# AM, KB and GL on VectorE alone, the first weights' words loaded at the start, and a reordered set-up in a planned recurrence-plus-FFN kernel

## The chip, the cores and the metric

The kernel runs on one core of a Trainium2 chip. The metric is device time in microseconds; several executions are timed and the median is given. One further execution was profiled, and every row below comes from it.

## The reference, cut to what matters

A recurrence over 768 steps for 4 x 8 independent heads with a 40 x 40 state, and two feed-forward layers over its 3072 output rows:

```python
for t in range(S):                       # S = 768, D = 40, B = 4, H = 8
    y[:, :, t] = einsum('bhd,bhde->bhe', r_t, state)
    Sa = einsum('bhde,bhe->bhd', state, a_t)
    state = state * w_t[:, :, None, :] - outer(Sa, b_t) + outer(v_t, k_t)
x = y.transpose(0, 2, 1, 3).reshape(3072, 320)
h = x @ w_in;  g = h * tanh(softplus(h)); x = g @ w_out      # 320 -> 2048 -> 320
h = x @ w_in2; g = h * cos(h);            out = g @ w_out2   # 320 -> 2048 -> 320
```

The weights arrive as 64-bit numbers, and are converted on the chip from their two 32-bit words.

## The kernel before, in words

The recurrence is cut into chunks of 32 steps. There are 48 chunks (`TOT`), numbered g: two halves of 16 heads, 24 chunks each. For each chunk there are four pieces of work.

- `pre(g)`: load `IN` (two DMAs), scan the decays on VectorE into `PE` (L662), take the reciprocal and scan back into `RP` (L667, L668), form `AM` (two products, L676) and `KB` (two products, L682), zero the other halves of `AM` on GpSimd (L689), multiply `AM` by `KB` on TensorE (L698), mask the result back into `AM` on VectorE (L708), and store the strictly triangular systems to DRAM (`l_d`, L721). `IN` has two buffers, `RP` and `KB` one.
- `inverse_two`: the systems of one to three chunks are read back with heads on partitions, and solved by 14 dependent pairs of VectorE instructions (L779 multiplies into `XT`, L777 adds into `XM`; both inputs of each lie in SBUF). The result goes to DRAM (`t_d`) and comes back as `TT`; `halves` joins the 16 x 16 blocks with `lowd` and `lowm`, two constants made in set-up. The first chunk alone uses `TMP` in place of `XM`.
- `chain(g)`: the serial part: small matmuls, evictions by ScalarE and VectorE (L708, L951, L978, L986), the state for the next chunk, and the output `Y`. Every fourth chunk stores a block of 256 rows to `x_d`.
- `prep` (first layer's weights): 17 loads of 512 KB of raw words into the five buffers `RW` (slices of `TMP`), two ScalarE instructions and four VectorE instructions of 128 x 512 each (L460 to L476), then a split into a high and a low part (`wih` and `wil`, L381 and L506); 5 further loads follow when `TMP` is given up.

`layer1(blk)` needs the output of chunk 4 blk + 3: it splits `XR` into `XH` (ScalarE, L1123) and `XL` (VectorE, L1125), runs the first product (L1068), the activation twice into `H` and `GH` (L1140, L1142), their difference `GL` (L1145), and the second product (L1049). There are 64 + 32 `GL` instructions. `layer2` does the same with another activation (its `GL` is L1231, on GpSimd). Its first two blocks have 256 rows, the others 512.

The order of the instructions of each engine is not written by hand. `Plan.run` is a list scheduler in Python: each piece is a `Task` with an engine or a choice of engines, an assumed duration, predecessors, buffers (`ring`) that it takes and frees, and a priority (`prio`, smaller goes first). The scheduler simulates the engines, and emits the instructions in the order in which it started the tasks. On the chip each engine then runs its list in that order, and waits by semaphores. `port=True` on a task says that VectorE and GpSimd tasks so marked are not planned at the same time. The planner has no bandwidth for DMA: it assumes a load to be there 2.6 to 4.1 us after its issue. Chains have the first priority (-10000 + 10 g), set-up apart; then inverses and `pre` (-5000 + 10 g); then the weights (-4921); then the layers (0 and up). All DMAs are issued by SP in one list.

What the change touches: `AMKB` and `GLE` are `("POOL", "DVE")`, so that the planner chooses GpSimd or VectorE for each; `B_G` biases that choice for GL; `W1_AFTER` makes all weight loads wait for the store of chunk 1's systems (`ldma[1]`); the list at L1263 hands out the five `RW` buffers, three of them after inverses of the first batches have been stored. In set-up, GpSimd does `setup_g` (constants, identity, masks), `setup_x` (zeroes `XM`) and `setup_tf` (`lowd`, and `lowm` as 16 additions one after the other) ahead of all other GpSimd work.

Of the kernel before, what the change touches and what calls it, by code (L numbers as in the profile page):

```python
# [14 lines left out]
ALU = mybir.AluOpType  # L15
# [31 lines left out]
       ("POOL", "POOL"): 0.1, ("POOL", "DVE"): 0.08, ("POOL", "PE"): 0.1, ("POOL", "ACT"): 0.1}  # L47
SLACK = {"PE": 0.02, "DVE": 0.02, "ACT": 0.02, "POOL": 0.2, "SP": 0.02}

EARLY = (20.0, 0.3)  # L50


class Task:
    __slots__ = ("eng", "dur", "fn", "preds", "acq", "rel", "aset", "lat", "prio", "end", "n_wait", "succ", "ready", "cols", "engs", "takes", "name", "durs", "bias", "ffn", "port", "mode", "soft")

    def __init__(self, eng, dur, fn, preds=(), acq=(), rel=(), aset=None, lat=None, prio=0.0, cols=0.0, bias=BIAS, port=False):
        self.bias = bias
        self.ffn = cols > 0 and prio >= 0
        self.cols = cols
        self.engs = (eng,) if isinstance(eng, str) else eng  # L60
        self.takes = fn.__code__.co_varnames[:1] == ("eng",)
        self.name = fn.__qualname__.replace("body.<locals>.", "").replace("<locals>.", "")
        self.durs = dict(zip(self.engs, dur if isinstance(dur, tuple) else (dur,) * len(self.engs)))
        dur = self.durs[self.engs[0]]
        self.eng, self.dur, self.fn, self.preds = self.engs[0], dur, fn, [p for p in preds if p is not None]
        self.acq, self.rel, self.aset, self.lat, self.prio = list(acq), list(rel), aset, lat, prio
        self.port = port
        self.mode = MODE.get(self.name, "full")
        self.soft = prio > -5500 and self.mode != "full" or self.name == "halves.mm.f"
        self.end, self.succ, self.ready = None, [], {e: 0.0 for e in self.engs}  # L70
        self.n_wait = 0
# [21 lines left out]
class Plan:  # L93
# [23 lines left out]
    def run(self):  # L117
# [10 lines left out]
        aset = None  # L128
# [6 lines left out]
        while done < len(self.tasks):  # L135
            best = None
            for e in self.ENGINES:
# [7 lines left out]
                for t in waiting[e]:  # L145
                    st = max(f, t.ready[e])
                    if t.port and e in ("DVE", "POOL"):
                        st = max(st, port_free)
                    ok = True
                    need = {}  # L150
                    for ring, *_ in t.acq:
                        need[ring] = need.get(ring, 0) + 1
                    for ring, n in need.items():
                        h = self.rings[ring]
                        if len(h) < n:
                            ok = False
# [24 lines left out]
                if pick is not None and (best is None or pick[1] < best[1]):
# [61 lines left out]
def body(ctx, tc, ins, out):  # L243
# [99 lines left out]

    def setup_tf():

        G.memset(lowd, 0.0)
        G.memset(lowm, 0.0)
        for i in range(4):
            r = slice(32 * i, 32 * i + 32)
            G.tensor_copy(lowd[r, 16:32], ident[r, 32 * i + 16:32 * i + 32])  # L350
        for i in range(16, 32):
            G.tensor_tensor(out=lowm, in0=lowm, in1=lowd[:, i:i + 1], op=ALU.add)

    def setup_x():
        for t in XL_m:
# [53 lines left out]
    DIRECT = 4  # L409
    C2_PRIO, B_HI2 = 4500.0, 1.0  # L410
    C2_AFTER = lambda wr: [t for w in wr[0] + wr[1] for t in w]
    AMKB, GLE = VG, VG
    HIE = EITHER
    HIE2, HID2 = ("ACT", "DVE"), (act(512, False), 0.34)
    LOE2, LOD2 = ("POOL", "DVE"), (pool(512), dve(512))
    B_CH, B_HI = 1.3, 0.6
    B_G = lambda blk: 0.6 if blk >= 8 else 3.0
    W1_AFTER = lambda: ldma[1]
    HOLD = ()
    W2_PRIO = 5e3  # L420
    G_POOL = lambda m: m % 2 == 1
# [216 lines left out]
    def fifo(name, t):  # L638
        p = prev_fifo.get(name)
        if p is not None:  # L640
            t.preds.append(p)
        prev_fifo[name] = t
        return t

    def pre(g):
# [28 lines left out]
        def am_f(p):  # L674
            r = slice(64 * p, 64 * p + 40)
            return lambda eng: EN[eng].tensor_tensor(out=am()[r, p], in0=sl(0)[r], in1=pe()[r, :, 0:C], op=ALU.mult)  # L676

        t_a0 = fifo("am", P.add(AMKB, (0.7, 0.33), am_f(0), preds=[t_sc, S_G], acq=[("AM", k("AM"))], prio=pr, port=True))
        t_a1 = P.add(AMKB, (0.7, 0.33), am_f(1), preds=[t_a0], prio=pr, port=True)

        def kb_f(j):
            return lambda eng: EN[eng].tensor_tensor(out=kb()[:, :, j], in0=sl(1 + j), in1=rp()[:, :, 1:], op=ALU.mult)  # L682

        t_k = fifo("kb", P.add(AMKB, (0.65, 0.33), kb_f(0), preds=[t_rp], acq=[("KB", k("KB"))], prio=pr, port=True))
        t_b = P.add(AMKB, (0.65, 0.33), kb_f(1), preds=[t_k, t_a1], rel=[k("RP"), k("IN")], prio=pr, port=True)

        def az_f(p):
            r = slice(64 - 64 * p, 128 - 64 * p)
# [422 lines left out]
    def layer1(blk, wready):  # L1111
# [18 lines left out]
        for quad in range(4):  # L1130
# [4 lines left out]
            for f in range(2):  # L1135
# [6 lines left out]
                gh = P.add("ACT", act(512), lambda hv=hv, key=key: A.activation(GH_t[P.at((key, "gh"))], hv(), AF.Mish),  # L1142
                           preds=[g], acq=[("GH", (key, "gh"))], rel=[(key, "h")], aset=MISH, prio=pr)
                g_prev[0] = gh
                gl = P.add(GLE, (1.27, dve(512)), lambda eng, f=f, Hv=Hv, key=key: EN[eng].tensor_tensor(  # L1145
                    out=GL_t[P.at((key, "gl"))], in0=Hv(f), in1=GH_t[P.at((key, "gh"))].bitcast(F32),
                    op=ALU.subtract), preds=[g, gh, l_prev[0]], acq=[("GL", (key, "gl"))],
                    rel=[(qk, ring)] if f == 1 else [], bias=B_G(blk), prio=pr, port=True)
                l_prev[0] = gl
                tlast = outs(1, blk, m, key, pr + 5, [gl, tlast] + wready[1][m], ("po1", blk), m == 0, m == 7)  # L1150
        last1[0] = tlast
# [97 lines left out]
    S_IN = [P.add("DVE", 1.1, lambda i=i: setup_in(i), prio=-1e6) for i in range(N_IN)]  # L1249
    S_D = P.add("DVE", 0.7, setup_d, prio=-9.5e5)  # L1250
    S_V = P.add("DVE", 2.0, setup_v, prio=-9e5)
    S_G = P.add("POOL", 6.6, setup_g, prio=-1e6)
    P.ring("TF", 1)
    S_TF = P.add("POOL", 4.9, setup_tf, preds=[S_G], prio=-8.9e5)
    S_X = P.add("POOL", 1.4, setup_x, prio=-9e5)
    state_init = {}
    W1_PREDS = []
    for g in range(TOT):
        load_step(g)
        pre(g)  # L1260
        if BT_OF[g][1] == BATCH[BT_OF[g][0]][1] - 1:
            inverse_two(BT_OF[g][0])
    for i, b in enumerate(((0, 1), (1, 2, 3), (3,), (), ())):  # L1263
        P.add("SP", 0.0, lambda i=i: P.grow("RW", [i], P.time), preds=[room_free[x] for x in b], lat=0.0, prio=-1e6)

    def half1():
# [148 lines left out]
```

## Time and profile before

| | |
|---|---|
| timed runs | 1185.69, 1184.59, 1175.63 us |
| median | 1184.59 us |
| profiled execution | 1186.17 us |
| its span, first to last instruction | 1184.4 us |
| TensorE busy in the span | 1060.9 us (90%) |
| VectorE, ScalarE, GpSimd busy | 816.4, 589.3, 458.9 us |
| mean granted TensorE clock | 0.965 |

The profiled execution's time is its span and 1.8 us around it. Busy time is the union of an engine's instructions; an instruction that is held up while it runs counts as busy. The three runs lie 0.85% apart, so that a difference under 1% can hardly be told from none.

### The profile page before, as it was taken

Reading aid. Unit: us, or ns where it says so; the run is one execution under the profiler, and the core shown is the slowest. Engines: PE = TensorE matmul, PEld = TensorE weight load, DVE = VectorE, ACT = ScalarE, POOL = GpSimd, SP = SyncE. Lnnn points to the kernel's source line nnn. Section 1 sums busy time; section 2 is a strip of 40 time slices with the busy share of each in tenths; the row PEclk is TensorE's granted clock in tenths of the full one; section 3 lists DMA queues with packets and bytes.
Section 4 is the critical chain, followed back from the end, with each engine's and each line's share of the span. In section 5 each row is a group of like instructions: output and inputs, shape, how many; then the busy total and the mean of one; then the engine's idle time right before and its main releaser. Section 6 shows DMA issues by size and latency. Waiting matters only on the chain. (4 is left out here: it accounts for less than half of the span.)

```text
span 1184.4 us, 37023 instructions
## 1 busy us (share of the span) xinstructions
PE 1060.9 (90%) x14888; PEld 962.3 (81%) x14888; DVE 816.4 (69%) x2158; ACT 589.3 (50%) x1477; POOL 458.9 (39%) x550
## 2 busy tenths in 40 slices
PE   2246798999999899899989999999999999999998
PEld 2245687878788788778778889999999999999997
DVE  6999899888888887899796643222655555555554
ACT  1356666456565265465545657433443444344333
POOL 7643555444443434344332117300333333333333
PEclk9999998989998889899898999999999999999999
DMA  4456565465555555465655645200110010000000
GB/s 117 117 155 192 160 174 149 118 166 137 166 147 159 147 139 141 141 183 151 162 143 135 172 120 176 73 26 26 41 39 12 19 32 24 26 25 13 12 12 23
DMA packets 116858, 123.45 MB, mean 104 GB/s; under 512 B 64848, under 2 KB 91216, under 8 KB 116688
## 3 DMA queue, kind: packets, MB, share of 16 engines
q1 hardware_dynamic: 116688, 121.10, 36.8%
q8 instruction: 117, 1.92, 0.7%
q14 instruction: 53, 0.43, 0.1%
HBM read 97.20 MB, written 23.86 MB: 102 GB/s over the span
## 5 line engine op out<-in xcount | busy, mean ns | idle before, releaser
L1231 POOL TENSOR_TENSOR GL<-H,GH 128x512 fp32r<-128x512 f32 x96 | 123.9, 1300 | 292.4 <-ACT GH L1229 256.8
L375 ACT ACTIVATE FL<-bank 64x160 f32<-64x160 f32 (+1 forms) x376 | 101.7, 295 | 141.3 <-PE bank L731 64.2
L1214 DVE TENSOR_SCALAR T<-bank 128x512 f32<-128x512 f32 x96 | 66.1, 688 | 123.6 <-PE bank L1083 110.8
L676 POOL TENSOR_TENSOR AM<-IN,PE 40x256 f32<-40x256 f32 x94 | 76.4, 812 | 189.1 <-DVE PE L662 59.7
L1221 ACT ACTIVATE T<-T,half_pi 128x512 f32<-128x512 f32 x96 | 69.0, 719 | 125.3 <-DVE T L1218 125.3
L1145 POOL TENSOR_TENSOR GL<-H,GH 128x512 fp32r<-128x512 f32 x64 | 84.9, 1334 | 100.7 <-ACT GH L1142 73.8
L779 DVE TENSOR_TENSOR XT<-XM 64x44 f32<-64x44 f32 (+9 forms) x322 | 104.6, 328 | 5.1 <-DMA XM<-l_d 2.7
L777 DVE TENSOR_TENSOR XM<-XM,XT 64x44 f32<-64x44 f32 (+9 forms) x322 | 98.4, 308 | 3.3
L1068 PE MATMUL bank<-XH,wih 128*128 128x256 f32 x448 | 97.5, 300 | 0.6 <-ACT GH L1142 0.5
L1140 ACT ACTIVATE H<-bank 128x512 f32<-128x512 f32 x96 | 57.4, 598 | 77.6 <-PE bank L1068 76.8
L1068 PE MATMUL bank<-XL,wih 128*128 128x256 f32 x448 | 90.8, 285 | 0.6 <-DVE XL L1125 0.6
L967 PE MATMUL bank<-FR,FL 104*64 104x72 f32 x1536 | 66.8, 243 | 26.5 <-DVE FR L951 11.5
L1068 PE MATMUL bank<-XH,wil 128*128 128x256 f32 x448 | 90.5, 284 | 0.0
L682 POOL TENSOR_TENSOR KB<-IN,RP 104x256 f32<-104x256 f32 x94 | 71.4, 777 | 41.6 <-PE bank L731 17.8
L967 PEld LDWEIGHTS bank<-FR,FL 104*64 104x64 f32 x1536 | 58.9, 149 | 34.7 <-issue 14.3
L1229 ACT ACTIVATE GH<-H 128x512 fp32r<-128x512 f32 x96 | 60.7, 632 | 51.1 <-DVE H L1223 37.0
L1145 DVE TENSOR_TENSOR GL<-H,GH 128x512 fp32r<-128x512 f32 x32 | 25.4, 792 | 82.3 <-ACT GH L1142 82.3
L1223 DVE TENSOR_TENSOR H<-bank,T 128x512 f32<-128x512 f32 x96 | 65.6, 684 | 18.2 <-ACT T L1221 18.1
L1068 PEld LDWEIGHTS bank<-XH,wih 128*128 128x128 f32 x448 | 70.7, 195 | 3.3 <-ACT GH L1142 0.9
L698 PE MATMUL bank<-AM,KB 104*64 104x64 f32 x768 | 37.6, 251 | 38.6 <-POOL AM L689 22.2
L1068 PEld LDWEIGHTS bank<-XL,wih 128*128 128x128 f32 x448 | 70.5, 194 | 0.9 <-DVE XL L1125 0.9
L1068 PEld LDWEIGHTS bank<-XH,wil 128*128 128x128 f32 x448 | 70.5, 194 | 0.0
(181 smaller groups left out, 3199.3 us busy)
## 6 DMA issues: line engine op xcount, KB each, us to landing
IN<-in_inT_dram SPq DMA_DIRECT2D x96, 161.4 KB
VR<-in_vR_dram SPq DMA_DIRECT2D x96, 160.0 KB
FR<-in_rI_dram SPq DMA_DIRECT2D x48, 180.0 KB
FR<-in_vF_dram SPq DMA_DIRECT2D x48, 144.0 KB
TMP<-in_w_in_dram SPq DMA_DIRECT2D x12, 512.0 KB
T<-in_w_in_dram SPq DMA_DIRECT2D x24, 256.0 KB
w_d<-T SPq DMA_DIRECT2D x44, 128.0 KB
AU<-w_d SPq DMA_DIRECT2D x22, 256.0 KB
```

The source lines that it names most:

```text
L375: A.activation(o, i, AF.Copy)
L676: return lambda eng: EN[eng].tensor_tensor(out=am()[r, p], in0=sl(0)[r], in1=pe()[r, :, 0:C], op=ALU.mult)
L682: return lambda eng: EN[eng].tensor_tensor(out=kb()[:, :, j], in0=sl(1 + j), in1=rp()[:, :, 1:], op=ALU.mult)
L777: V.tensor_tensor(out=b[:, 0:i, i + 1:16], in0=b[:, 0:i, i + 1:16], in1=tv, op=ALU.add)
L779: V.tensor_tensor(out=tv, in0=bc(b[:, i:i + 1, i + 1:16], (2 * n, i, w)), in1=bc(b[:, 0:i, i:i + 1], (2 * n, i, w)), op=ALU.mult)
L967: PE.matmul(fp[64 * p:64 * p + 64, qp], fl()[0:104, n * D:n * D + 64], fr()[:, n], start=True, stop=True)
L1068: PE.matmul(hp[:, f], pss[i][0], pss[i][1], start=(i == 0), stop=(i == 7))
L1145: gl = P.add(GLE, (1.27, dve(512)), lambda eng, f=f, Hv=Hv, key=key: EN[eng].tensor_tensor(out=GL_t[P.at((key, "gl"))], in0=Hv(f), in1=GH_ ...
L1214: a = P.add("DVE", dve(512), lambda f=f, hv=hv, Tv=Tv: V.tensor_scalar(out=Tv(f), in0=hv(), scalar1=0.25, scalar2=MAGIC, op0=ALU.add, op1= ...
L1221: c = P.add("ACT", act(512, False, 1), lambda f=f, Tv=Tv: A.activation(Tv(f), Tv(f), AF.Sin, scale=-TWO_PI, bias=half_pi), preds=[b], aset ...
L1223: gt = P.add("DVE", dve(512), lambda f=f, Tv=Tv, Hv=Hv, hv=hv: V.tensor_tensor(out=Hv(f), in0=hv(), in1=Tv(f), op=ALU.mult), preds=[c, g_f ...
L1231: gl = P.add("POOL", pool(512), lambda f=f, Hv=Hv, key=key: G.tensor_tensor(out=GL_t[P.at((key, "gl"))], in0=Hv(f), in1=GH_t[P.at((key, "g ...
```

## The change

- AM and KB (`am_on`) and layer 1's GL (`GLE`) have VectorE as their only engine; `B_G` goes.
- `setup_tf` goes to VectorE with a priority of -4970, and makes `lowm` by a tree of four additions in place of 16; `setup_x` stays on GpSimd, but with priority -4970.
- `W1_AFTER` gives nothing, and four of the five `RW` buffers are free at time 0; the first waits only for the inverse of chunk 0, which uses its space.
- The planner's rule for VectorE's first 20 us (`EARLY`: an important task that can start within 0.3 us goes ahead of one that can start now) goes; the slack is 0.02 us throughout. A new field `pull` is 0 for all tasks, and changes nothing.

```diff
-EARLY = (20.0, 0.3)
+PULL, PULL_INV, PULL_CH = 0.0, 0, 0
...
-                    key = (max(st, f + (EARLY[1] if e == "DVE" and f < EARLY[0] else SLACK[e])), rank, t.prio + (5e4 if sw else 0), order[id(t)])
+                    key = (max(st - t.pull if e == "DVE" else st, f + SLACK[e]), rank, t.prio + (5e4 if sw else 0), order[id(t)])
...
-        G.memset(lowd, 0.0)
-        G.memset(lowm, 0.0)
+        V.memset(lowd, 0.0)
         for i in range(4):
             r = slice(32 * i, 32 * i + 32)
-            G.tensor_copy(lowd[r, 16:32], ident[r, 32 * i + 16:32 * i + 32])
-        for i in range(16, 32):
-            G.tensor_tensor(out=lowm, in0=lowm, in1=lowd[:, i:i + 1], op=ALU.add)
+            V.tensor_copy(lowd[r, 16:32], ident[r, 32 * i + 16:32 * i + 32])
+        tmp = TB[:, 0]
+        V.tensor_tensor(out=tmp[:, 0:8], in0=lowd[:, 16:24], in1=lowd[:, 24:32], op=ALU.add)
+        V.tensor_tensor(out=tmp[:, 8:12], in0=tmp[:, 0:4], in1=tmp[:, 4:8], op=ALU.add)
+        V.tensor_tensor(out=tmp[:, 12:14], in0=tmp[:, 8:10], in1=tmp[:, 10:12], op=ALU.add)
+        V.tensor_tensor(out=lowm, in0=tmp[:, 12:13], in1=tmp[:, 13:14], op=ALU.add)
...
-    AMKB, GLE = VG, VG
+    am_on, GLE = lambda g, d: ("DVE", 0.33), ("DVE",)
...
-    B_G = lambda blk: 0.6 if blk >= 8 else 3.0
-    W1_AFTER = lambda: ldma[1]
+    W1_AFTER = lambda: None
...
-        t_a0 = fifo("am", P.add(AMKB, (0.7, 0.33), am_f(0), preds=[t_sc, S_G], acq=[("AM", k("AM"))], prio=pr, port=True))
+        t_a0 = fifo("am", P.add(*am_on(g, 0.7), am_f(0), preds=[t_sc, S_G], acq=[("AM", k("AM"))], prio=pr, port=True))
...
-        t_k = fifo("kb", P.add(AMKB, (0.65, 0.33), kb_f(0), preds=[t_rp], acq=[("KB", k("KB"))], prio=pr, port=True))
+        t_k = fifo("kb", P.add(*am_on(g, 0.65), kb_f(0), preds=[t_rp], acq=[("KB", k("KB"))], prio=pr, port=True))
...
-                gl = P.add(GLE, (1.27, dve(512)), lambda eng, f=f, Hv=Hv, key=key: EN[eng].tensor_tensor(
+                gl = P.add(GLE, (dve(512),), lambda eng, f=f, Hv=Hv, key=key: EN[eng].tensor_tensor(
...
-    S_G = P.add("POOL", 6.6, setup_g, prio=-1e6)
+    S_G = P.add("POOL", 6.9, setup_g, prio=-1e6)
     P.ring("TF", 1)
-    S_TF = P.add("POOL", 4.9, setup_tf, preds=[S_G], prio=-8.9e5)
-    S_X = P.add("POOL", 1.4, setup_x, prio=-9e5)
+    S_TF = P.add("DVE", 1.2, setup_tf, preds=[S_G], prio=-4.97e3)
+    S_X = P.add("POOL", 1.1, setup_x, prio=-4.97e3)
...
-    for i, b in enumerate(((0, 1), (1, 2, 3), (3,), (), ())):
+    for i, b in enumerate(((0,), (), (), (), ())):
```

## Rows read from the trace of the kernel before

**Rows 1.** The page: span, and busy time by engine.

```profile
span 1184.4 us, 37023 instructions
...
PE 1060.9 (90%) x14888; PEld 962.3 (81%) x14888; DVE 816.4 (69%) x2158; ACT 589.3 (50%) x1477; POOL 458.9 (39%) x550
```

**Rows 2.** Windows: length; PE, PEld, DVE, ACT, POOL busy; clock, DMA share, GB/s.

```profile
0.00:30.00 30.00, 7.77 (x108) 6.25 (x108) 19.48 (x50) 4.52 (x14) 23.19 (x82) 1.00 0.42 121
30.00:140.00 110.00, 56.66 (x1407) 47.57 (x1405) 104.05 (x282) 60.24 (x157) 52.57 (x57) 1.00 0.57 162
140.00:180.00 40.00, 36.26 (x596) 32.22 (x596) 34.48 (x94) 26.91 (x69) 19.83 (x25) 1.00 0.56 156
180.00:650.00 470.00, 431.03 (x8543) 381.46 (x8543) 397.44 (x1264) 258.82 (x775) 197.83 (x260) 0.91 0.55 148
650.00:1184.40 534.40, 529.23 (x4246) 494.76 (x4244) 260.95 (x471) 238.85 (x463) 165.50 (x126) 1.00 0.16 49
```

**Rows 3.** XH's line L1068: ns min/median/max, first and last start in us.

```profile
L1068 PE MATMUL bank<-XH,wih x448: 276/281/582, 139.9 to 880.1; 128*128 128x256 f32 x150
```

**Rows 4.** Timeline of the start: start us, us, instruction, idle time before it.

```profile
8.68 0.83 DVE L676 TENSOR_TENSOR AM<-IN,PE 40x256 f32<-40x256 f32 x2
9.52 0.76 DVE L682 TENSOR_TENSOR KB<-IN,RP 104x256 f32<-104x256 f32 x2
10.09 5.18 POOL L352 TENSOR_TENSOR lowm<-lowm,lowd 128x1 f32<-128x1 f32 x16
...
16.05 1.12 PE L698 MATMUL bank<-AM,KB 104*64 104x64 f32 x16 [16.05 <-POOL AM L689]
...
25.07 0.83 SPq L448 DMA_DIRECT2D TMP<-in_w_in_dram  x2
...
30.80 0.66 ACT L453 ACTIVATE T<-TMP 128x512 f32<-128x512 f32 x1 [3.23 <-DMA TMP<-in_w_in_dram]
```

**Rows 5.** DMA view, 0 to 30 us: slices of 0.75 us; issues, KB.

```profile
GB/s 0 0 0 0 132 242 66 58 127 147 251 181 164 192 182 193 198 182 39 0 0 0 0 0 0 44 44 77 242 192 16 73 74 115 127 237 219 279 317 415
...
TMP<-in_w_in_dram SPq DMA_DIRECT2D x2, 512.0 KB
```

**Rows 6.** GpSimd's groups, 180 to 650 us: busy us, mean ns, idle before.

```profile
L1145 POOL TENSOR_TENSOR GL<-H,GH 128x512 fp32r<-128x512 f32 x52 | 69.6, 1345 | 53.4 <-ACT GH L1142 43.5 <-issue 3.1 <-PE bank L967 2.7
L676 POOL TENSOR_TENSOR AM<-IN,PE 40x256 f32<-40x256 f32 x68 | 54.7, 804 | 176.0 <-DVE PE L662 52.8 <-DVE XM L777 42.8 <-PE bank L874 20.2
L682 POOL TENSOR_TENSOR KB<-IN,RP 104x256 f32<-104x256 f32 x70 | 52.0, 762 | 35.7 <-PE bank L731 16.5 <-issue 7.4 <-DVE XM L777 7.4
```

**Rows 7.** VectorE's groups: GL at 760 to 830 us, inverse at 180 to 650.

```profile
L1145 DVE TENSOR_TENSOR GL<-H,GH 128x512 fp32r<-128x512 f32 x18 | 12.5, 692 | 48.0 <-ACT GH L1142 48.0
...
L779 DVE TENSOR_TENSOR XT<-XM 64x56 f32<-64x56 f32 (+6 forms) x252 | 84.1, 336 | 4.7 <-DMA XM<-l_d 2.7
L777 DVE TENSOR_TENSOR XM<-XM,XT 64x56 f32<-64x56 f32 (+6 forms) x252 | 77.6, 310 | 2.8
```

**Rows 8.** The same lines and L708: ns min/median/max of one.

```profile
L777 DVE TENSOR_TENSOR XM<-XM,XT x322: 133/194/4045, 42.3 to 660.9; 64x56 f32<-64x56 f32 x23, 64x54 f32<-64x54 f32 x23, 64x50 f32<-64x50 f32 x22, 64x44 f32<-64x44 f32 x22
...
L779 DVE TENSOR_TENSOR XT<-XM x322: 145/195/4017, 41.5 to 660.7; 64x56 f32<-64x56 f32 x23, 64x54 f32<-64x54 f32 x23, 64x50 f32<-64x50 f32 x22, 64x44 f32<-64x44 f32 x22
...
L708 DVE TENSOR_TENSOR AM<-bank,maskG x192: 253/285/296, 17.3 to 638.0; 64x128 f32<-64x128 f32 x192
```

**Rows 9.** Timeline at 341 us, GpSimd and VectorE.

```profile
340.89 2.99 POOL L1145 TENSOR_TENSOR GL<-H,GH 128x512 fp32r<-128x512 f32 x2
...
341.23 1.28 DVE L779 TENSOR_TENSOR XT<-XM 64x50 f32<-64x50 f32 x1
...
342.65 1.29 DVE L777 TENSOR_TENSOR XM<-XM,XT 64x50 f32<-64x50 f32 x1
```

**Rows 10.** GpSimd's groups in the first 140 us.

```profile
L676 POOL TENSOR_TENSOR AM<-IN,PE 40x256 f32<-40x256 f32 x20 | 17.0, 851 | 11.4 <-DVE PE L662 6.9 <-DVE TMP L779 3.2 <-DVE TMP L777 0.6
L682 POOL TENSOR_TENSOR KB<-IN,RP 104x256 f32<-104x256 f32 x19 | 16.0, 856 | 4.5 <-DVE XM L777 2.7 <-POOL AM L676 0.8 <-DVE AM L708 0.5
```

More of the change, by code (lines that the diff above doesn't have):

```diff
@@ L48 @@
 SLACK = {"PE": 0.02, "DVE": 0.02, "ACT": 0.02, "POOL": 0.2, "SP": 0.02}
-EARLY = (20.0, 0.3)
+PULL, PULL_INV, PULL_CH = 0.0, 0, 0
 class Task:
-    __slots__ = ("eng", "dur", "fn", "preds", "acq", "rel", "aset", "lat", "prio", "end", "n_wait", "succ", "ready", "cols", "engs", "takes", "name", "durs", "bias", "ffn", "port", "mode", "soft")
+    __slots__ = ("eng", "dur", "fn", "preds", "acq", "rel", "aset", "lat", "prio", "end", "n_wait", "succ", "ready", "cols", "engs", "takes", "name", "durs", "bias", "ffn", "port", "mode", "soft", "pull")
     def __init__(self, eng, dur, fn, preds=(), acq=(), rel=(), aset=None, lat=None, prio=0.0, cols=0.0, bias=BIAS, port=False):
@@ L67, in __init__ @@
         self.port = port
+        self.pull = PULL if prio < PULL_CH or (prio < PULL_INV and "inverse_two.step" in self.name) else 0.0
         self.mode = MODE.get(self.name, "full")
@@ L676, in am_f @@
             return lambda eng: EN[eng].tensor_tensor(out=am()[r, p], in0=sl(0)[r], in1=pe()[r, :, 0:C], op=ALU.mult)
-        t_a0 = fifo("am", P.add(AMKB, (0.7, 0.33), am_f(0), preds=[t_sc, S_G], acq=[("AM", k("AM"))], prio=pr, port=True))
-        t_a1 = P.add(AMKB, (0.7, 0.33), am_f(1), preds=[t_a0], prio=pr, port=True)
+        t_a0 = fifo("am", P.add(*am_on(g, 0.7), am_f(0), preds=[t_sc, S_G], acq=[("AM", k("AM"))], prio=pr, port=True))
+        t_a1 = P.add(*am_on(g, 0.7), am_f(1), preds=[t_a0], prio=pr, port=True)
         def kb_f(j):
             return lambda eng: EN[eng].tensor_tensor(out=kb()[:, :, j], in0=sl(1 + j), in1=rp()[:, :, 1:], op=ALU.mult)
-        t_k = fifo("kb", P.add(AMKB, (0.65, 0.33), kb_f(0), preds=[t_rp], acq=[("KB", k("KB"))], prio=pr, port=True))
-        t_b = P.add(AMKB, (0.65, 0.33), kb_f(1), preds=[t_k, t_a1], rel=[k("RP"), k("IN")], prio=pr, port=True)
+        t_k = fifo("kb", P.add(*am_on(g, 0.65), kb_f(0), preds=[t_rp], acq=[("KB", k("KB"))], prio=pr, port=True))
+        t_b = P.add(*am_on(g, 0.65), kb_f(1), preds=[t_k, t_a1], rel=[k("RP"), k("IN")], prio=pr, port=True)
         def az_f(p):
@@ L1144, in layer1 @@
                 g_prev[0] = gh
-                gl = P.add(GLE, (1.27, dve(512)), lambda eng, f=f, Hv=Hv, key=key: EN[eng].tensor_tensor(
+                gl = P.add(GLE, (dve(512),), lambda eng, f=f, Hv=Hv, key=key: EN[eng].tensor_tensor(
                     out=GL_t[P.at((key, "gl"))], in0=Hv(f), in1=GH_t[P.at((key, "gh"))].bitcast(F32),
                     op=ALU.subtract), preds=[g, gh, l_prev[0]], acq=[("GL", (key, "gl"))],
-                    rel=[(qk, ring)] if f == 1 else [], bias=B_G(blk), prio=pr, port=True)
+                    rel=[(qk, ring)] if f == 1 else [], prio=pr, port=True)
                 l_prev[0] = gl
```

## The prediction

> **What bounds the kernel now.** I read the busy times first, then the stages. TensorE is busy 1060.9 of 1184.4 us [rows 1], and the change gives it no work and takes none. So the time is that work plus TensorE's idle time, 123 us, plus what a low clock adds. The windows view says where the idle time lies [rows 2]: 22 us in the first 30, 53 us from 30 to 140, 4 us from 140 to 180, 39 us from 180 to 650, and 5 us in all the rest. The first feed-forward matmul starts at 139.9 us [rows 3]. This makes three stages. Until 140 us only the recurrence is there, and TensorE waits for it. From 140 to 650 us the chunks go on and layer 1 fills what they leave. After 650 us TensorE is full (529 of 534 us), so nothing that this change moves can be worth anything there.
>
> In the first stage VectorE is the bound: 104 of 110 us from 30 to 140 [rows 2]. In the first 30 us it is busy only 19.5 us. What is late there is GpSimd's set-up: the 16 additions into lowm run from 10.1 to 15.3 us, the zeroing of AM stands behind them, and the first matmul of chunk 0 starts at 16.05 us, released by that zeroing [rows 4]. In the second stage TensorE is busy 92%, VectorE 85%. The granted clock is 0.91 there on the mean [rows 2], so parts of the stage ran at the lower of its two levels, 1.2 GHz in place of 2.4. At most 0.09 x 470 = 42 us is lost to it; the change does not act on it directly, and I keep it at no change.
>
> **Moving AM, KB and GL, in the second stage.** From 180 to 650 us GpSimd runs 68 AM, 70 KB and 52 GL instructions [rows 6]. On VectorE two AM take 0.83 us and two KB 0.76 us at 8.7 us [rows 4], and one GL takes 692 ns where GpSimd is mostly idle [rows 7]. The added work is 68 x 0.415 + 70 x 0.38 + 52 x 0.692 = 28 + 27 + 36 = 91 us. VectorE has 470 - 397 = 73 us idle there [rows 2], so by this sum alone it would not fit.
>
> But VectorE's busy time holds time in which it is stopped. The two instructions of the inverse have a median of 195 and 194 ns, a longest of 4 us [rows 8], and means of 336 and 310 ns in this stage [rows 7]. The timeline shows why: while GpSimd runs two GL, one L779 and one L777 of the usual size take 1.28 and 1.29 us [rows 9]. L708, with one input in PSUM, stays at 253 to 296 ns in all its 192 instances [rows 8], so it is the second SBUF input that is held up. What comes back is 252 x (336 - 195) + 252 x (310 - 194) = 36 + 29 = 65 us, and some more from other instructions with two SBUF inputs, which I leave out. The net is 91 - 65 = +26 us against 73 us idle. That fits, with VectorE at 90% in place of 85%. GpSimd keeps the zeroing of AM, which only writes, and a few weight splits.
>
> The Trainium skill, SBUF — State Buffer, section "Who interferes with whom", states that a VectorE instruction with two SBUF inputs and a GpSimd instruction that reads SBUF exclude each other for a whole instruction. The rows on the 1.28 us and on L708 agree with it. By the rule the return is full, and the net stays the +26 us worked out above.
>
> What does the second stage gain? TensorE idles 39 us in it, 8 us of every 100. The chunks do not wait long for AM and KB there: GpSimd itself idles 176 us before AM, and GL waits for GH [rows 6]. So the shorter latency (AM 804 to 415 ns, GL 1345 to 692 ns) lies mostly beside other work, and no TensorE stall of note is removed. The gain is in VectorE's order holding closer to plan. Its ends are -10 us (a quarter of the 39 us goes) and +19 us (see the third rival). I take -3 us, near the end at which little happens, since the rows show VectorE neither the cause nor free.
>
> **The set-up.** Without the 16 additions the zeroing of AM can start at 10.1 us at the latest, in place of 15.3, and without the copies and the zeroing of XM ahead of them earlier still. Then KB ends last, at 10.28 us [rows 4], and chunk 0's first matmul could start at 10.3 us: 5.8 us earlier. The tree on VectorE is ten short instructions. The trace has none of that size on VectorE; the nearest, the inverse's smallest, take 133 to 145 ns [rows 8], giving about 1.3 us; the ends are 0.7 and 2.6 us (L708's 253 ns each). Nobody needs lowm before the first join of blocks, after the first inverse, so it can fill a gap. The zeroing of XM on GpSimd is needed later still, and GpSimd is free: nothing.
>
> **The words ahead.** Before, the first two loads are issued at 25.1 us, and ScalarE gets the first words at 30.8 us [rows 4]. Now four buffers are free at time 0. By the order of priorities SP issues one load ahead of chunk 0's IN, both INs, and then three loads, before SV, FR and VR, which wait for VectorE's memsets. VectorE's 10.5 idle us of the first 30 [rows 2] can then take conversion steps, and the weights are done earlier. I count half of the gaps, 5 us, since the words come in only as the queue lets them.
>
> The queue is the price. From 8.25 to 13.5 us it carries 164 to 198 GB/s, seven slices in a row without a gap [rows 5]; at 185 a load of 512 KB [rows 5] takes 2.8 us, and four take 11 us. All DMAs are in SP's list. What moves before from 3 to 14.25 us (the slices add up to 2354, times 0.75 us: 1.77 MB) are the inputs of the first chunks. With 2.1 MB of words that is 3.9 MB, 21 us at 185 GB/s, so the queue would be full until about 23 us. The store of chunk 0's systems, issued 5.8 us earlier, would stand in it; before, the queue was empty from 14.25 to 18.75 us [rows 5], just ahead of that store. So the set-up's 5.8 us are given back, between none and all of it; I take all but 1 us.
>
> The Trainium skill, DMA: Bandwidth & Descriptors, section "Queues, rings and completion order", has each DMA engine consume descriptors in ring order, though later ones may finish earlier. That speaks against the change; the second rival is what it would do here at its worst.
>
> **AM and KB in the first stage.** 20 AM and 19 KB [rows 10] cost VectorE 20 x 0.415 + 19 x 0.38 = 15.5 us there, and the row sums 1.3 us. Returned are 65/176 us per us of GpSimd's time, the ratio of the second stage (176 us is the sum of its three groups in rows 6), of the 33 us in rows 10: 12 us. Net +5 us, against the 5 us of filled gaps. What is left is the 1 us of set-up, and the latency of AM and KB: together 1.6 us a chunk [rows 4] in place of 2 x 0.851 + 2 x 0.856 = 3.4 us [rows 10]. For the three chunks that gate the second inverse that is up to 3 x 1.8 = 5.4 us; VectorE being full, I take 2 us. The first stage gives -3 us, between -14 and +14.
>
> **Sum.** -3 - 3 = -6 us. On the profiled execution, 1186.2 to 1180; on the median of the runs, 1.6 us below it, 1184.6 to 1178.6. I say 1178 us.
>
> **Rivals.** *Everything shows.* The queue keeps up, chunk 0 gains its 5.8 us, VectorE's gaps are filled with 8 us of conversions, and TensorE's idle time in the second stage falls by 6 us: -20 us, 1165 us. For it: DMA stands still from 14.25 to 18.75 us [rows 5], and VectorE is 95% busy from 30 to 140 us [rows 2], so each us taken off its list counts. Against it: the four loads come just when the queue is full.
>
> *The queue stops VectorE.* The planner believes words to be there 4.1 us after issue; two took 5.7 us [rows 4], and four need 11 us. If conversion steps are put ahead of pre(1) to pre(3) on VectorE, the whole recurrence stands behind words that have not landed: up to 11 us, added one for one as TensorE has nothing else before 140 us, with 3 us of VectorE's added work: +14 us, 1199 us. It decides once VectorE's waits for words and late INs in the first 25 us come to more than the 5.8 us won in set-up.
>
> *VectorE is full.* If less than 18 of the 65 us come back, 91 us do not fit into 73 us, and the chunks slow; nothing returned means 18 us too much, and some waiting: up to +19 us, 1204 us. Against it stands rows 9.
>
> *Nothing.* VectorE's sum in the first stage is unchanged, and the rest hides beside TensorE: 1184 us.
>
> **How the numbers follow.** About 1% (12 us) is what a measurement here can tell. The forecast has 0.39 (between 1168 and 1188; 0.06 of it faster by over 1%, 0.33 within). Everything shows: 0.31 (0.29 faster, 0.02 within). Nothing: 0.11, within. The queue stops VectorE: 0.13 (0.11 slower, 0.02 within). VectorE full: 0.06 (0.05 slower, 0.01 within). Together faster 0.35, within 1% 0.49, slower 0.16. The range leaves out the strong end of the first rival below 1157 us and the upper ends of the slow ones above 1200 us, together under 2 in 10. The forecast's own range is 1168 to 1188 us.
>
> **What would show it.** Right: medians and means of L777 and L779 close together, GpSimd nearly empty until 650 us, VectorE about 90% busy from 180 to 650 us, the first L698 before 12 us, the queue without a gap up to some 23 us, the first L1068 between 132 and 142 us. Wrong: VectorE idle behind L453's words or IN in the first 25 us (second rival); L1068 before 130 us (first rival); TensorE's idle time from 180 to 650 us above 50 us or below 30 us. A clock in the second stage that moves by 0.03 or more would shift the time by some 14 us that no step here accounts for, and make the number wrong with the reasons right.

## The result, and the profile after

The changed kernel takes 1146.7 us (median of 4 runs, 1143.9 to 1151.7) against 1185.1 us in the runs beside it: a ratio of 0.971, interval 0.964 to 0.978. The prediction said 1178 us, within 1157 to 1200: the result lies below that range. The experiments below ran in other sessions, where the kernel before had medians of 1178 to 1180 us and the changed kernel was not timed again; each is given by its ratio to the runs of before on its own chip. Since the medians of before alone differ by 7 us, differences between medians of two sessions are not read below that.

The page of the changed kernel: span, busy time, and the granted clock in 40 slices.

```profile
span 1146.4 us, 36936 instructions
...
PE 1036.4 (90%) x14888; PEld 943.0 (82%) x14888; DVE 827.0 (72%) x2422; ACT 588.1 (51%) x1474; POOL 225.1 (20%) x276
...
PEclk9999988999999989999999999999999999999999
```

Its windows view, in the stages of [rows 2]: length; busy time of PE, PEld, DVE, ACT, POOL; clock; DMA share, GB/s.

```profile
0.00:30.00 30.00, 5.48 (x72) 4.28 (x72) 26.04 (x66) 10.69 (x22) 12.36 (x52) 1.00 0.61 185
30.00:140.00 110.00, 63.04 (x1488) 53.99 (x1488) 103.45 (x313) 58.68 (x156) 26.28 (x26) 1.00 0.51 148
140.00:180.00 40.00, 29.84 (x468) 26.46 (x468) 38.17 (x120) 25.39 (x66) 12.18 (x19) 0.81 0.59 160
180.00:650.00 470.00, 446.80 (x9472) 397.15 (x9473) 419.87 (x1540) 280.60 (x847) 19.03 (x62) 0.98 0.58 162
650.00:1146.40 496.40, 491.19 (x3396) 461.11 (x3392) 239.50 (x387) 212.78 (x385) 155.25 (x118) 1.00 0.13 39
```

The span fell by 38.0 us. TensorE's instructions are as many as before, yet its busy time fell by 24.5 us, from 1060.9 [rows 1] to 1036.4; its idle time fell by 13.5 us. The stages say where. From 180 to 650 us the idle time went from 39.0 [rows 2] to 470 - 446.8 = 23.2 us, and the clock from 0.91 to 0.98, so that the time lost to the lower level went from at most 0.09 x 470 = 42 to at most 9 us. From 140 to 180 us both got worse: idle 3.7 to 10.2 us, and up to 0.19 x 40 = 8 us lost to the clock where nothing was. The clock terms together are -33 + 8 = -25 us at these bounds: they answer to the 24.5 us of busy time. Up to 140 us the idle time fell from 75.5 to 71.5 us, 4 us.

VectorE's groups of the changed kernel from 180 to 650 us that the change bears on, with busy us, mean ns and idle time before, and GpSimd's only group there:

```profile
L780 DVE TENSOR_TENSOR XM<-XM,XT 64x50 f32<-64x50 f32 (+6 forms) x262 | 48.4, 185 | 2.4
L782 DVE TENSOR_TENSOR XT<-XM 64x50 f32<-64x50 f32 (+6 forms) x262 | 48.4, 185 | 2.0
L1148 DVE TENSOR_TENSOR GL<-H,GH 128x512 fp32r<-128x512 f32 x58 | 39.4, 680 | 7.0 <-ACT GH L1145 6.9
L685 DVE TENSOR_TENSOR KB<-IN,RP 104x256 f32<-104x256 f32 x69 | 28.3, 411 | 0.0
L679 DVE TENSOR_TENSOR AM<-IN,PE 40x256 f32<-40x256 f32 x68 | 28.2, 414 | 1.0
```

```profile
L692 POOL MEMSET AM<- 64x256 f32 x62 | 19.0, 307 | 384.4 <-issue 293.8 <-PE bank L877 88.9
```

One line of the inverse over the whole run (ns min/median/max, first and last start):

```profile
L782 DVE TENSOR_TENSOR XT<-XM x322: 134/188/1190, 48.0 to 623.5; 64x14 f32<-64x14 f32 x22, 64x50 f32<-64x50 f32 x22, 64x56 f32<-64x56 f32 x22, 64x54 f32<-64x54 f32 x22
```

The two instructions of the inverse, 310 and 336 ns on the mean before [rows 7], now take 185 ns each, and L782's longest is 1.2 us where its line had 4.0 [rows 8]. Added are 39.4 + 28.3 + 28.2 = 96 us; VectorE's busy time in this stage rose by only 22.4 us.

The start, in the timeline and by XH's line:

```profile
10.13 0.16 DVE L356 TENSOR_TENSOR lowm<-TB 128x1 f32<-128x1 f32 x1
...
13.43 1.12 PE L701 MATMUL bank<-AM,KB 104*64 104x64 f32 x16 [13.43 <-DVE KB L685]
...
17.17 0.71 DVE L665 TENSOR_TENSOR_SCAN PE<-IN,D 104x264 f32<-104x264 f32 x1 [1.06 <-DMA IN<-in_inT_dram]
...
L1071 PE MATMUL bank<-XH,wih x448: 276/281/582, 133.1 to 841.9; 128*128 128x256 f32 x150
```

Chunk 0's first matmul starts 2.6 us earlier than before, at 13.4 us: VectorE's row sums end at 10.3 us and push chunk 0's KB back, which ends last. The first layer-1 matmul starts at 133.1 in place of 139.9 us [rows 3].

The DMA view of the first 30 us, in slices of 0.75 us:

```profile
GB/s 0 0 98 246 246 252 215 225 202 262 311 344 410 389 204 247 235 223 216 165 215 242 203 74 3 5 169 355 254 3 0 50 176 264 102 46 44 158 317 224
```

### The profile page after: what moved, and what is told of

It is laid out like the page before. It is cut to its first block, busy times and chain, and to the rows that moved or that the text cites. A ratio compares the mean times of both kernels' runs of the same rounds, so it can differ in the third digit from the quotient of the medians.

```text
span 1146.4 us, 36936 instructions
## 1 busy us (share of the span) xinstructions
PE 1036.4 (90%) x14888; PEld 943.0 (82%) x14888; DVE 827.0 (72%) x2422; ACT 588.1 (51%) x1474; POOL 225.1 (20%) x276
## 4 chain that ended last, share of the span: by engine, by line
PE 52%; DVE 11%; DMA 4%; issue 3%; ACT 2%; SPq 1%; POOL 0%; ACTq 0%; DVEq 0%; POOLq 0%
PE bank L1086 12%; PE bank L1102 11%; PE bank L1052 11%; PE bank L1071 11%; PE bank L970 2%; DVE SV L981 1%; DMA TT<-t_d 1%; DVE XM L780 1%; DVE AM L711 1%; DVE XT L782 1%; PE bank L946 1%; DVE GL L1148 1%; DMA XR<-x_d 1%; PE bank L1193 1%; DVE FR L954 1%
## 5 line engine op out<-in xcount | busy, mean ns | idle before, releaser
L1234 POOL TENSOR_TENSOR GL<-H,GH 128x512 fp32r<-128x512 f32 x96 | 124.0, 1300 | 294.2 <-ACT GH L1232 258.9
L379 ACT ACTIVATE FL<-bank 40x160 f32<-40x160 f32 (+1 forms) x376 | 101.6, 295 | 101.8 <-PE bank L1013 51.7
L1148 DVE TENSOR_TENSOR GL<-H,GH 128x512 fp32r<-128x512 f32 x96 | 70.4, 733 | 86.7 <-ACT GH L1145 86.3
L692 POOL MEMSET AM<- 64x256 f32 x96 | 29.4, 307 | 386.1 <-issue 293.8
L970 PE MATMUL bank<-FR,FL 104*64 104x72 f32 x1536 | 68.2, 243 | 11.9 <-issue 3.5
L970 PEld LDWEIGHTS bank<-FR,FL 104*64 104x64 f32 x1536 | 59.5, 148 | 19.7 <-issue 7.3
L701 PEld LDWEIGHTS bank<-AM,KB 104*64 104x64 f32 x768 | 30.9, 155 | 53.1 <-issue 50.5
L1071 PE MATMUL bank<-XH,wix 128*128 128x256 f32 x224 | 68.8, 307 | 0.0
L1221 DVE SCALAR_TENSOR_TENSOR T<-T,bank 128x512 f32<-128x512 f32 x96 | 65.5, 682 | 1.6
L1052 PE MATMUL bank<-woh1a,GH 128*128 128x320 f32 x192 | 65.8, 343 | 0.0
```

What stands on the lines that cost most here:

```text
L379: A.activation(o, i, AF.Copy)
L701: PE.matmul(gp[c0:c0 + 64, q // 2], kb()[:, q].rearrange("p a t -> p (a t)"), am()[0:104, :, q], start=True, stop=True)
L970: PE.matmul(fp[64 * p:64 * p + 64, qp], fl()[0:104, n * D:n * D + 64], fr()[:, n], start=True, stop=True)
L1052: PE.matmul(o, l[:, f, tsl], r, start=(first and f == 0 and i == 0), stop=(last and f == 1 and i == 2))
L1071: PE.matmul(hp[:, f], pss[i][0], pss[i][1], start=(i == 0), stop=(i == 7))
L1148: gl = P.add(GLE, (dve(512),), lambda eng, f=f, Hv=Hv, key=key: EN[eng].tensor_tensor(out=GL_t[P.at((key, "gl"))], in0=Hv(f), in1=GH_t[P.a ...
```

## The experiments

The theory after the result: *contention*. GpSimd instructions that read SBUF (the on-chip memory of the engines) stop VectorE's instructions with two SBUF inputs; VectorE falls behind its plan, the chunks slow, TensorE gets idle time and a lower clock between 180 and 650 us. Rivals: *start-up* (words and set-up carry the gain), *plan* (a lucky order), *latency* (AM, KB and GL are merely shorter on VectorE).

**The old engines in the new order.** The changed kernel; only the engine at issue differs, so that no list of another engine is re-planned.

```diff
-return lambda eng: EN[eng].tensor_tensor(out=am()[r, p], ...)          # and kb_f alike
+return lambda eng: EN["POOL" if g else eng].tensor_tensor(out=am()[r, p], ...)
-gl = ... EN[eng].tensor_tensor(out=GL_t[...
+gl = ... EN["POOL" if blk < 8 else eng].tensor_tensor(out=GL_t[...
```

> The changed kernel with its plan, so the order of every other engine is unchanged, but the AM and KB of chunks 1 to 47 and the GL of layer 1's first eight blocks (64 of 96) are issued to GpSimd in place of VectorE. Contention theory (GpSimd reading SBUF stops VectorE's two-input instructions, these stops leave TensorE without dense work, and the clock falls): most of the 38 us comes back, 1170 to 1195 us, means of the inverse's two instructions at 300 ns or more, clock from 180 to 650 us at 0.94 or less. Start-up theory (the words ahead and the set-up carry the gain): 1145 to 1160 us, since both are kept. Plan theory (the new order is merely a lucky one): within 1% of 1147 us.

Measured 1205.3 us, ratio 1.022 (1.019 to 1.025): 58 us above the changed kernel, and slower than before. Windows view from 180 to 650 us, and VectorE's inverse there:

```profile
180.00:650.00 470.00, 416.30 (x8321) 367.35 (x8322) 405.43 (x1221) 245.43 (x743) 189.72 (x257) 0.92 0.53 145
...
L780 DVE TENSOR_TENSOR XM<-XM,XT 64x14 f32<-64x14 f32 (+6 forms) x244 | 83.6, 344 | 3.8
L782 DVE TENSOR_TENSOR XT<-XM 64x26 f32<-64x26 f32 (+6 forms) x243 | 80.6, 332 | 4.7 <-DMA XM<-l_d 1.1
```

The inverse is back at 344 and 332 ns, the clock at 0.92, TensorE's idle time at 53.7 us. The words and the set-up were kept, so start-up does not carry the gain. The loss is larger than expected, and TensorE's waits in this stage (us in total, times, longest) say why:

```profile
PE bank L701 <- POOL KB L685: 12.8, 7, 6.9
PE bank L1052 <- POOL GL L1148: 12.2, 11, 2.5
```

In an order planned for VectorE, TensorE waits 25 us for GpSimd's later results: that is *latency*, beside the stops. In the kernel before, whose order was planned with GpSimd's durations, the same view has no wait of TensorE for GpSimd.

**The move alone, on the kernel before.**

```diff
-    AMKB, GLE = VG, VG
+    am_on, GLE = lambda g, d: ("DVE", 0.33), ("DVE",)
```

> The kernel before with one part of the change alone: AM, KB and layer 1's GL have VectorE as their only engine. Set-up, the words' time and the early slack are as before. Contention theory: 1150 to 1165 us, clock from 180 to 650 us at 0.96 or more, the inverse's two instructions at a mean under 230 ns. Start-up theory: 1175 to 1190 us. Plan theory: anything from 1150 to 1200 us, with no tie to the clock.

Measured 1159.0 us, ratio 0.984 (0.980 to 0.987). From 180 to 650 us and by the first layer-1 matmul:

```profile
180.00:650.00 470.00, 443.16 (x9444) 391.74 (x9443) 419.90 (x1533) 280.86 (x847) 22.09 (x69) 0.98 0.59 162
...
L1068 PE MATMUL bank<-XH,wih x448: 276/281/582, 151.9 to 852.4; 128*128 128x256 f32 x150
```

The second stage is that of the changed kernel. The start has got worse: layer 1 begins 12 us later than before, at 151.9 us.

**The words late again.** The changed kernel with two lines undone.

```diff
-    W1_AFTER = lambda: None
+    W1_AFTER = lambda: ldma[1]
-    for i, b in enumerate(((0,), (), (), (), ())):
+    for i, b in enumerate(((0, 1), (1, 2, 3), (3,), (), ())):
```

> The changed kernel with the weights' words loaded as before: after the store of chunk 1's systems, and three of the five buffers handed out after inverses of the first batches. Contention theory: the start is some 3 to 7 us later, 1149 to 1156 us, clock as in the changed kernel (0.98). Start-up theory: 1165 to 1185 us. First layer-1 matmul at 136 to 141 us in place of 133.

Measured 1158.4 us, ratio 0.984 (0.980 to 0.987). Layer 1 begins at 145.8 us, later than expected:

```profile
L1071 PE MATMUL bank<-XH,wih x448: 276/281/582, 145.8 to 852.4; 128*128 128x256 f32 x150
```

So the early words are worth 13 of the 19 us between the move alone (151.9) and the whole change (133.1). It is not shown that the conversion itself is late: in this run the last part of `wih` was ready at 133.2 us, `wil` at 134.8 and XH at 123.5, and the first layer-1 matmul stood behind chunk work in TensorE's list until 145.8. What the words moved is, in part at least, the planned order.

**The old set-up, and the early slack.** Two runs: lowd, lowm and XM's zeroing back on GpSimd ahead of all else; the 0.3 us rule back.

```diff
-    S_TF = P.add("DVE", 1.2, setup_tf, preds=[S_G], prio=-4.97e3)
-    S_X = P.add("POOL", 1.1, setup_x, prio=-4.97e3)
+    S_TF = P.add("POOL", 4.9, setup_tf, preds=[S_G], prio=-8.9e5)      # with its old body
+    S_X = P.add("POOL", 1.4, setup_x, prio=-9e5)
...
-f + SLACK[e]
+f + (EARLY[1] if e == "DVE" and f < EARLY[0] else SLACK[e])
```

> The changed kernel with the set-up as before: lowd and lowm (16 additions) and the zeroing of XM on GpSimd ahead of all else. Contention theory: 1145 to 1152 us, the first chunk matmul near 16 us in place of 13.4, and little of that left at 133 us. Start-up theory: 1155 us or more.

> The changed kernel with the planner's rule for VectorE's first 20 us back (0.3 us of slack for important tasks), the last part of the change not yet tried alone. Contention theory: within 1% of 1147 us, as the rule touches only the first 20 us. If the early order matters as much as the words and the set-up (8 to 12 us each): 1155 to 1162 us.

Measured 1154.9 us (0.979, 0.976 to 0.982; expected up to 1152) and 1156.2 us (0.981, 0.976 to 0.986). In both, layer 1 begins no later than in the changed kernel, though chunk 0's first matmul starts at 20.4 us in the first and at 10.7 us in the second:

```profile
20.41 1.12 PE L699 MATMUL bank<-AM,KB 104*64 104x64 f32 x16 [20.41 <-POOL AM L690]
...
L1069 PE MATMUL bank<-XH,wih x448: 276/281/582, 130.8 to 844.9; 128*128 128x256 f32 x150
```

```profile
10.65 1.12 PE L702 MATMUL bank<-AM,KB 104*64 104x64 f32 x16 [10.65 <-DVE lowd L349]
...
L1072 PE MATMUL bank<-XH,wih x448: 276/281/562, 131.6 to 846.2; 128*128 128x256 f32 x150
```

So their 8 and 9 us do not come by a later layer 1, and the set-up's path as I had predicted it is refuted: a first matmul 7 us later or 3 us earlier than in the changed kernel leaves layer 1's start where it is. The losses are hardly larger than what sessions differ by, or another order alone does.

**Another order.** Seed 31 in place of 97 for the planner's 1% jitter of durations, in both kernels.

> The changed kernel with another seed (31 in place of 97) for the planner's 1% jitter of assumed durations: another order, same work on the same engines. Contention theory: 1140 to 1162 us, at least 15 us under the same seed's kernel before. Plan theory: 1150 to 1190 us, overlapping it.

> The kernel before with seed 31. Contention theory: 1170 to 1195 us. Plan theory: 1150 to 1190 us, not reliably above the changed kernel with this seed.

Measured 1152.8 us (0.979, 0.974 to 0.984) for the changed kernel and 1197.1 us (1.017, 1.010 to 1.024) for the one before; from 180 to 650 us in this order:

```profile
180.00:650.00 470.00, 445.55 (x9453) 394.00 (x9452) 417.61 (x1538) 279.63 (x843) 18.98 (x62) 0.99 0.60 161
```

```profile
180.00:650.00 470.00, 426.42 (x8630) 376.16 (x8631) 394.34 (x1274) 260.06 (x781) 193.93 (x258) 0.92 0.56 150
```

This one other order is worth 6 us in the changed kernel (no more than sessions differ by) and 18 in the one before, and the two stay 44 us apart. In these four the clock goes with the engines, not with the seed. Plan is out as the main cause, and sets the size below which a re-planned part cannot be read: the 12 us that the move alone and the late words lose against the changed kernel are of that size too.

**GL or AM and KB.** First with the planner's choice given back for one of them.

```diff
-    am_on, GLE = lambda g, d: ("DVE", 0.33), ("DVE",)
+    am_on, GLE = lambda g, d: ("DVE", 0.33), VG        # first run; B_G as before
+    AMKB, GLE = VG, ("DVE",)                           # second run
```

> The changed kernel with the planner's choice between GpSimd and VectorE given back for layer 1's GL alone (bias as before); AM and KB stay on VectorE. Contention theory: GL's part of GpSimd's 176 us from 180 to 650 us was 70, so about 40% of what the move gave: 1153 to 1162 us, clock 0.95 to 0.97 there. Plan theory: not tied to how many GL go to GpSimd, anything within 1.5% of 1147 us.

> The changed kernel with the choice given back for AM and KB alone; layer 1's GL stays on VectorE. Contention theory: about 60% of what the move gave: 1156 to 1168 us, clock 0.94 to 0.97 from 180 to 650 us. Plan theory: anything within 1.5% of 1147 us.

Measured 1171.0 us (0.993, 0.989 to 0.997) and 1175.8 us (0.997, 0.993 to 1.001). Both lose more than expected. The second run's reason is another one than expected:

```profile
180.00:650.00 470.00, 431.93 (x8791) 383.60 (x8793) 405.54 (x1443) 256.21 (x785) 90.58 (x120) 0.92 0.56 151
```

```profile
180.00:650.00 470.00, 441.68 (x9536) 388.46 (x9535) 411.79 (x1384) 275.23 (x838) 134.67 (x204) 0.98 0.59 160
...
L780 DVE TENSOR_TENSOR XM<-XM,XT 64x44 f32<-64x44 f32 (+6 forms) x259 | 65.8, 254 | 2.5
...
L1071 PE MATMUL bank<-XH,wih x448: 276/281/562, 169.3 to 865.5; 128*128 128x256 f32 x150
```

GL's choice costs in the second stage (idle 38 us, clock 0.92). With the choice for AM and KB the clock stays at 0.98 and the idle time at 28 us although the stops are back (254 ns), so stops need not end in a lower clock; the loss lies at the start: the planner's new order lets layer 1 begin at 169.3 us. So the same two on GpSimd without a new order:

```diff
-EN[eng]
+EN["POOL" if blk < 8 else eng]    # GL alone: first run
+EN["POOL" if g else eng]          # AM and KB alone: second run
```

> The changed kernel, plan and order the same, with GL of layer 1's first eight blocks issued to GpSimd; AM and KB stay on VectorE. Contention theory: 1165 to 1185 us, clock from 180 to 650 us 0.92 to 0.95, the inverse's two instructions at a mean of 220 ns or more. Latency theory: the same time or less of a loss, but equal to nothing in the run with reads beside GL.

> The changed kernel, plan and order the same, with AM and KB from chunk 1 on issued to GpSimd; GL stays on VectorE. Contention theory: 1165 to 1190 us; with the GL run the two losses add up to about the 58 us of both together. If the loss of AM and KB was the re-planned start alone (first layer-1 matmul at 169 us when the planner had the choice): 1147 to 1158 us, the first layer-1 matmul before 138 us.

Measured 1178.1 us (1.001, 0.997 to 1.005) and 1169.0 us (0.995, 0.991 to 0.998): 31 and 22 us above the changed kernel, 53 together against 58 for both at once. The profiled executions took 1171.8 us (among the first run's fastest) and 1175.4 us (the second's slowest), so their stages are not to be compared with each other. In their order, with TensorE's waits for GpSimd:

```profile
180.00:650.00 470.00, 433.71 (x8992) 385.23 (x8993) 420.97 (x1458) 266.98 (x806) 94.91 (x119) 0.95 0.57 154
...
L780 DVE TENSOR_TENSOR XM<-XM,XT 64x26 f32<-64x26 f32 (+6 forms) x266 | 67.0, 252 | 3.0
...
PE bank L701 <- POOL AM L692: 0.2, 1, 0.2
```

```profile
180.00:650.00 470.00, 431.77 (x8937) 383.30 (x8937) 414.12 (x1368) 264.34 (x797) 135.08 (x208) 0.95 0.57 155
...
PE bank L701 <- POOL KB L685: 13.2, 7, 7.0
```

With GL on GpSimd the inverse is at 252 ns, and TensorE waits 0.2 us for GpSimd: this loss is not latency as the trace shows it. With AM and KB there, 13 us of waits for KB stand beside the stops.

**Reads and writes of no use.** The changed kernel with more work on GpSimd, into a tile that nothing uses: products of the identity, or memsets.

```diff
+    def extra():
+        for _ in range(2):                                      # memsets: range(4)
+            G.tensor_tensor(out=SCR, in0=ident, in1=ident, op=ALU.mult)   # G.memset(SCR, 0.0)
...
+                if g: extra()             # behind each AM and KB; two calls beside each GL, blk < 8
```

> The changed kernel, plan and order the same, with extra instructions on GpSimd that nobody waits for: two products of the identity with itself (128 x 128) into an unused tile beside each AM and KB instruction from chunk 1 on, and four beside each GL of the first eight blocks. They read SBUF and lie on no path, so this is contention alone, without GpSimd's latency. Contention theory: L782 and L780 (the inverse) rise to means of 270 ns or more, clock from 180 to 650 us falls to 0.95 or less, 1165 to 1200 us. Latency theory (what the move gave is the shorter wait for AM, KB and GL, not the end of the stops): 1145 to 1153 us.

> As the run with extra reads, but the extra instructions are memsets of the same unused tile (four beside each AM and KB, eight beside each GL): they only write SBUF. Contention theory with GpSimd's reads as the cause: no change, 1144 to 1153 us, the inverse's means under 220 ns. If any GpSimd work in this place costs (a full GpSimd list that delays the zeroing of AM): the same time as with extra reads.

Measured 1214.9 us (1.030, 1.023 to 1.037) with reads, 1151.6 us (0.976, 0.971 to 0.981) with writes. From 180 to 650 us, reads and then writes:

```profile
180.00:650.00 470.00, 414.06 (x8212) 365.35 (x8213) 428.83 (x1409) 247.14 (x745) 311.14 (x573) 0.93 0.53 144
...
L380 POOL TENSOR_TENSOR SCR<-ident 128x128 f32<-128x128 f32 x499 | 288.3, 578 | 36.1
...
L795 DVE TENSOR_TENSOR XT<-XM 64x14 f32<-64x14 f32 (+6 forms) x245 | 60.0, 246 | 1.7
```

```profile
180.00:650.00 470.00, 442.74 (x9412) 393.05 (x9412) 420.16 (x1541) 278.80 (x840) 236.40 (x1111) 0.99 0.60 162
...
L380 POOL MEMSET SCR<- 128x128 f32 x1043 | 217.6, 209 | 58.0
...
L795 DVE TENSOR_TENSOR XT<-XM 64x44 f32<-64x44 f32 (+6 forms) x263 | 48.6, 185 | 3.2 <-DMA XM<-l_d 1.1
```

This pair decides whether reads alone can do it. 288 us of them raise the inverse's L795 to 246 ns and take the clock to 0.93 and TensorE's idle time to 56 us; 218 us of writes leave all three nearly where they were (185 ns, 0.99, 27 us). Both stand in GpSimd's list beside the zeroing of AM, and TensorE's weight loads waited for them a little in this stage, 3.8 us with reads and 6.0 with writes, so that is not the difference. The amount is larger than the 176 us of the kernel before [rows 6], so the size needs a third run, with one call beside each GL only:

> The changed kernel, plan and order the same, GL on VectorE, with two products of the identity on GpSimd (578 ns each in the run with extra reads, 1.16 us together against GL's 1.28) beside each GL of the first eight blocks, waited for by nobody. Contention theory: a loss of at least half of that of GL on GpSimd in the same order. Latency theory: 1144 to 1154 us.

Measured 1160.3 us (0.985, 0.979 to 0.991), 14 us above the changed kernel; GL itself on GpSimd costs 31. That is 0.44 of GL's loss, under the half that contention was expected to give, and above what latency allowed.

```profile
180.00:650.00 470.00, 435.56 (x9241) 385.61 (x9241) 426.00 (x1523) 272.27 (x823) 95.28 (x184) 0.98 0.58 158
...
L791 DVE TENSOR_TENSOR XT<-XM 64x50 f32<-64x50 f32 (+6 forms) x262 | 51.2, 195 | 3.2 <-DMA XM<-l_d 1.2
```

But this run does not price GL's stops. Its reads wait for nothing, so GpSimd runs them behind the zeroing of AM and not when GL would run, and they hardly stop the inverse: 195 ns, where GL brought it to 252. What share of GL's 31 us the stops are stays open.

**The hole at chunk 8.** An attempt at a better kernel: the weights' priority behind pre of chunks 8 to 10.

```diff
-    wr1 = prep(1, ("w_in", "w_out"), None, -4921.0, [W1_AFTER()], ...
+    wr1 = prep(1, ("w_in", "w_out"), None, -4895.0, [W1_AFTER()], ...
```

> The changed kernel with the first layer's weights at priority -4895 in place of -4921, so that pre of chunks 8 to 10 goes ahead of them on VectorE. In the changed kernel chunk 8's F product starts 47 us after chunk 7's (214 against 168 us), and the clock is at its lower level for 20 us between 140 and 185 us. If that hole costs TensorE time: 1138 to 1145 us, with chunk 8 before 195 us. If the weights were what the hole paid for: the first layer-1 matmul 4 us or more later, and 1147 to 1155 us.

Measured 1168.1 us, ratio 0.993 (0.988 to 0.997), some 21 us above the changed kernel and above both ranges expected. Layer 1 begins at 150.6 us, and the second stage is worse too:

```profile
180.00:650.00 470.00, 432.27 (x9196) 380.71 (x9194) 407.58 (x1497) 273.08 (x823) 25.07 (x68) 0.95 0.59 159
...
L1071 PE MATMUL bank<-XH,wih x448: 276/281/582, 150.6 to 867.9; 128*128 128x256 f32 x150
```

The inverse is at 184 ns here, so this kernel's lower clock is not from stops. A layer 1 that starts late goes with a longer time here and in the runs above that have it; why the second stage suffers was not followed up.

## Why the prediction was wrong

**The step that failed** is the end of its first part: "the change does not act on it directly, and I keep it at no change", of the clock, with its echo in "no TensorE stall of note is removed ... I take -3 us". From 180 to 650 us the runs show -16 us of idle time and up to -33 us of clock where -3 us stood. In that stage the changed kernel had 23 us of idle time at a clock of 0.98; with the old engines in its order it had 54 us at 0.92, with reads of no use 56 us at 0.93. So the change did act on the clock; that it did so by TensorE's idle time is what these rows suggest, and no run varied the one without the other. I had the bound, 42 us, on the page and set it aside; even the lower end I gave (-10 us) held nothing for the clock. The stall was in the trace as well, TensorE's wait for VectorE's `FR`, an eviction of the chain (180 to 650 us, before and then after):

```profile
PE bank L967 <- DVE FR L951: 10.2, 6, 2.1
```

```profile
PE bank L970 <- DVE FR L954: 0.6, 2, 0.4
```

And GpSimd's 176 us of idle time ahead of AM, which I read as slack, were for over half waits for VectorE's scan and inverse, 52.8 and 42.8 us [rows 6]. The last part did name a clock that moves by 0.03 as a way to be wrong; it moved by 0.07.

**Right, with sizes.** That GpSimd's reads stop VectorE, that 65 us or more would return, and that VectorE would be at 90%: it is at 419.9 of 470, 89%, with 96 us added and a net of +22.4 where +26 was forecast. The rule of the Trainium skill (SBUF — State Buffer, "Who interferes with whom") is borne out by the run with writes: a GpSimd instruction that only writes does not stop VectorE (185 ns). What I did not see is that TensorE can wait less for VectorE while VectorE's sum goes up. My reading, not tested apart, is that a stop delays whatever stands behind it in a fixed order, the chunks' own instructions among them.

**The queue** (second rival) was sized too dear. It moved from 1.5 to 17.25 us the 3.9 MB that I had counted, at 245 GB/s in place of 185, and was empty by 18 us, not 23. VectorE waited 1.06 us for an IN and not at all for words (ScalarE did, up to 3.8 us at a time), and the rival's 14 us did not come.

**The start.** -3 us was forecast, 4 us of idle time went before 140 us, and layer 1 began at 133.1 us, inside the 132 to 142 us given. But the terms were others, and the agreement is in part luck. The set-up's first matmul gained 2.6 us of the 5.8, and undoing the set-up or the slack leaves layer 1's start where it is. Going by layer 1's start, the words are worth 13 us and the move costs 12; I had them at 5 us and the move at +5. From 140 to 180 us up to 14 us were lost, which I did not foresee: chunk 8's product (L970) comes 47 us after chunk 7's.

**The rivals.** The first ("everything shows", 1165 us, 0.31) had the direction and less idle time of TensorE (6 us of the 16), not the clock; its sign, layer 1 before 130 us, did not come. "VectorE is full" and "nothing" are refuted. Of my own signs, the first L698 before 12 us and the full queue up to 23 us did not come, and one of being wrong did: TensorE's idle time of 23 us is below the 30 named.

**Still open.** The parts do not add up exactly, since most are re-plans, and another order was worth 6 to 18 us: the 8 and 9 us of set-up and early slack cannot be told from that. The loss does not follow the stops in proportion. By their means above 185 ns, the inverse's two instructions lost some 74 us of the second stage with the old engines, 28 with reads of no use, 34 with GL alone, 34 with AM and KB alone and 5 with reads beside GL; the whole times rose by 58, 68, 31, 22 and 14 us. The stops and the latency of AM and KB were not tried apart, and neither were the chunks' pace and GL's in the clock's return.

## What to carry to other kernels

Where TensorE is not at its higher clock throughout, a change that makes its feeders more even can be worth more than the idle time in the trace: take 1 minus the granted clock, times the stage, into the range as a bound, and not only the gaps. It is no price by itself: seven executions of the kernel before had a mean granted clock of 0.936 to 0.945 and took 1174 to 1182 us, while those at 0.965 to 0.977 took 1166 to 1186. Compare an instruction's mean with its median before adding work to an engine: VectorE had 65 us of stops to give back, and taking GpSimd's reads away paid for work that did not fit by the sum. To learn what a shared resource costs, add work that nobody waits for, once of the suspected kind and once of the harmless kind, and look in the trace whether it runs at the moments meant.

## What the runs showed of the hardware that I had not expected

GpSimd's memsets did not stop VectorE's inverse even in number: 1043 of them, 218 us in 470, left it at 185 ns, where 499 products (288 us) brought it to 246. The products were drawn out as well: over the run the shortest takes 389 ns and the median 402, and the mean in that stage is 578. That fits two engines that hold each other up both ways; what held up a given product was not followed. The DMA queue moved 245 GB/s over 15.75 us of the start with the words in it, where I had taken 185, and 389 to 410 GB/s in two slices; before, its best slice in the first 20 us was 251, though 415 came at 29.25 us [rows 5].
